# Theta from the attention output and a product of w_o and w_theta, with that output kept in DRAM

## The chip, the cores and the metric

The kernel runs on one core of a Trainium2 chip. The metric is the device time of one execution in microseconds; of several runs the median is given. Inputs and outputs lie in the core's DRAM; the host only lays arrays out.

## The reference

Three blocks follow each other, for four batches of 576 tokens and 512 channels. First, banded attention: eight heads of 64, each token looks at the 64 tokens up to itself. Second, four attention experts with causal masks over the result x, of which each token uses the two with the largest gate: `out = sum_e gate_e * (a_e @ v_e @ wo_e)`. Third, a mixing block over that output, called x again:

```
theta = x @ w_theta
zr, zi = x * cos(theta), x * sin(theta)
y = w_tok_r @ zr + w_tok_i @ zi        (over tokens)
u = x + y
out = u + max(u @ w_ch, 0)             (over channels)
```

The second block's output is linear in the gated attention outputs: with O of width 256 (four experts of 64) and w_o of 256 x 512, x = O w_o, and so theta = O (w_o w_theta). The first form contracts over 512, the second over 256.

## The kernel before

Everything is float32. A product is made from three matmuls (`mm3`, lines 92 to 95): each operand is split by `split` (lines 85 to 90) into a high part, rounded to the type fp32r, and the rest, and high x high, high x low and low x high are accumulated in one bank of PSUM. `split` uses two engines: ScalarE (ACT) casts the high part, and VectorE (DVE) or GpSimd (POOL) subtracts. TensorE writes to banks with the tags as, ta, g, bs and tb (one, one, two, two and two).

The program is written as generators that `merge` (line 45) interleaves by costs and totals (`KN`); the order of its text is the order of priority. A planner then sets the order of the instructions on every engine and queue with a simulated timeline (`schedule_with_timeline_sim`), so that work which is ready can go ahead of earlier text. Within an engine and within SP's queue of DMA issues the resulting order is fixed. Waits on the device follow from the tiles: a tile in a tag with one buffer can be written once all readers of the last tile of that tag are done.

The stages per batch b are: `phase_a(b)` is the banded attention, which loads q, k and v through SP (lines 231 to 248); `qk(b, ep)` and `vg_gates(b)` make the experts' q, k, v and gates; `attn(b, ep)` is the causal attention of a pair of experts, in five tiles t of tokens. Its result, already weighted by the gates and transposed (128 channels by 576 tokens), is split at line 487 into `oh` and `ol` (three buffers each). `wo(b)` multiplies with w_o and leaves the result in `x2T[b]`, 4 x 128 channels by 576 tokens. Attention of batch b is merged with phase_a of the next ones, wo of the one before and the conversion of the weights, which come as 64-bit floats and pass through ACT, DVE and POOL (`load64`).

The mixing block is in the last stages. `x_split(b)` (line 514) splits x2T[b] for tokens 0 to 511 into the eight tiles cx, casts on ACT, subtractions on POOL, and once per pair of batches gathers the last 64 tokens of both in `xt` and splits them. `theta(b, dh)` (line 527) goes over four token tiles of 128 (five where the pair's tail is due) for one half dh of the channels: per tile 12 matmuls of 256 columns against w_theta (`wth`, `wtl`), two transposes of x, then rounding on DVE, sine and cosine on ACT, and z with its split. `mix(b, dh)` sums over tokens in four banks, nine steps of 12 matmuls of 288 columns; four adds on DVE (line 599) empty the banks. `channel(b)` is the product with w_ch and the output's stores. `theta(b, 1)` is merged with `mix(b, 0)`, `theta(b+1, 0)` with `mix(b, 1)`; then comes `channel(b)`. `theta(0, 0)` is merged with `wo(3)`, the last part of the attention stages (line 712).

Of the kernel before, what the change touches and what calls it, by code (L numbers as in the profile page):

```python
# [11 lines left out]
F32 = mybir.dt.float32  # L12
# [45 lines left out]
def kernel(ctx, tc, qT, kT, vw, consts, w_in, w_o, w_th, w_tk, w_ch, outT):  # L58
# [10 lines left out]
    halfpi = cp.tile([P, 1], F32, name="halfpi")  # L69
    nc.gpsimd.memset(halfpi, math.pi / 2.0)  # L70

    wth = cp.tile([P, NC, DM], F32R, name="wth")
    wtl = cp.tile([P, NC, DM], F32R, name="wtl")
    x2T = {b: cp.tile([P, NC, S], F32, name=f"x2T{b}") for b in range(2)}

    BANKS = {"as": 1, "ta": 1, "g": 2, "bs": 2, "tb": 2}
# [330 lines left out]
    def attn(b, ep):  # L407
# [7 lines left out]
        for t in range(5):  # L415
# [69 lines left out]
                          pT[:, j, i, :m], start=(j == t - 1), stop=False)  # L485
            nc.tensor.matmul(o[:, :m], VD[ep][:, t].rearrange("p h d -> p (h d)"), pT[:, t, 0, :m], start=(t == 0), stop=True)
            split(oh[:, q0 : q0 + m], ol[:, q0 : q0 + m], o[:, :m], nc.scalar, nc.vector)
            yield 0.4 * (t + 1)

    def wo(b):  # L490
# [10 lines left out]

    HW = DM // 2
    NK0 = 5
    xtags = ["QS0", "QS1", "KA0", "KA1", "KL0", "oh", "ol", "KL1"]
    utags = ["QS2", "QS3", "KA2", "KA3", "oh", "ol", "oh", "ol"]
    XH, Z, UH, XT, W4 = {}, {}, {}, {}, 4 * P
    nz = [0]

    def hl_set(tags, name):
        t = [bp.tile([P, S], F32R, tag=tag, bufs=3 if tag in ("oh", "ol") else 1, name=f"{name}{i}")  # L510
             for i, tag in enumerate(tags)]
        return t[0::2], t[1::2]

    def x_split(b):
        XH[b] = hl_set(xtags, f"cx{b}")
        for c in range(NC):
            split(XH[b][0][c][:, :W4], XH[b][1][c][:, :W4], x2T[b][:, c, :W4], nc.scalar, nc.gpsimd)
        if b % 2 == 0:
            xt = kp.tile([P, NC, P], F32, tag="xt", name=f"xt{b}")
            for k in range(2):  # L520
                pool_mul(xt[:, :, 64 * k : 64 * k + 64], x2T[b + k][:, :, W4:], 1.0)
            xth = kp.tile([P, NC, P], F32R, tag="xth", name=f"xth{b}")
            xtl = kp.tile([P, NC, P], F32R, tag="xtl", name=f"xtl{b}")
            split(xth, xtl, xt, nc.scalar, nc.gpsimd)
            XT[0] = xt, xth, xtl

    def theta(b, dh):
        x2 = x2T[b]
        xh, xl = XH[b]
        dsl = slice(dh * HW, dh * HW + HW)  # L530
        for i in range(4 if b % 2 else 5):
            n = f"{b}{dh}{i}"
            if i < 4:
                tok = slice(i * P, i * P + P)
                x32, lh, ll = (lambda c: x2[:, c, tok]), (lambda c: xh[c][:, tok]), (lambda c: xl[c][:, tok])
            else:
                xt, xth, xtl = XT[0]
                x32, lh, ll = (lambda c: xt[:, c]), (lambda c: xth[:, c]), (lambda c: xtl[:, c])
            th = bank([P, HW], "bs", f"th{n}")
            for c in range(NC):  # L540
                mm3(th, lh(c), ll(c), wth[:, c, dsl], wtl[:, c, dsl], c == 0, c == NC - 1)
            xk = bank([P, HW], "tb", f"xk{n}")
            for c in range(2):
                nc.tensor.transpose(xk[:, c * P : (c + 1) * P], x32(2 * dh + c), ident)
            if i % 2 == 0:
                ang = bp.tile([P, 2, 2, HW], F32, tag="bms", bufs=2, name=f"ang{n}")
            rn, sn = ang[:, i % 2, 0], ang[:, i % 2, 1]
            nc.vector.tensor_scalar(out=rn, in0=th, scalar1=MAGIC, scalar2=-MAGIC,
                                    op0=ALU.add, op1=ALU.add)
            nc.vector.tensor_sub(out=rn, in0=th, in1=rn)  # L550
            nc.scalar.activation(out=sn, in_=rn, func=AF.Sin, scale=TWO_PI)  # L551
            nc.scalar.activation(out=rn, in_=rn, func=AF.Abs)
            nc.scalar.activation(out=rn, in_=rn, func=AF.Sin, bias=halfpi, scale=-TWO_PI)  # L553
            if i < 4:
                if b > 0 and nz[0] % NZ == 6:
                    zt = rp.tile([P, 2, 2, HW], F32R, tag="bmsx", name=f"z{n}")
                else:
                    pool, tag = ((cp, "zc"), (rp, "wtu"), (bp, "bpT"))[nz[0] % NZ % 6 // 2]
                    zt = pool.tile([P, 2, 2, HW], F32R, tag=tag, bufs=2, name=f"z{n}")
                nz[0] += 1  # L560
                if b > 0 and nz[0] < 14:
                    nz[0] = 14
                Z[b, dh, i] = zt
                for q, tr in enumerate((rn, sn)):
                    z = rp.tile([P, HW], F32, tag="z", bufs=2, name=f"zf{n}{q}")
                    nc.vector.tensor_mul(out=z, in0=xk, in1=tr)  # L566
                    split(zt[:, q, 0], zt[:, q, 1], z, nc.scalar, nc.gpsimd)
            else:
                for k in range(2):
                    zt = kp.tile([P, 1, 2, HW], F32R, tag=f"zt{k}{dh}", name=f"z{n}{k}")  # L570
                    Z[b + k, dh, i] = zt
                    z = rp.tile([P, HW], F32, tag="z", bufs=2, name=f"zf{n}{k}")
                    r = slice(64 * k, 64 * k + 64)
                    for q, tr in enumerate((rn, sn)):
                        nc.vector.tensor_mul(out=z[64 * q : 64 * q + 64], in0=xk[r], in1=tr[r])
                    split(zt[:, 0, 0], zt[:, 0, 1], z, nc.scalar, nc.gpsimd)
            yield 1.5
# [91 lines left out]
    for b in range(B):  # L669
        todo = [(KN["AT"][2 * b], attn(b, 0)), (KN["QK"][2 * b], qk(b, 1))]  # L670
        if KN["WOI"] == 2 * b:
            todo.append((KN["CW"][6], load_w(w_o, 2, lambda c: woh[c], lambda c: wol[c], "zc")))
        if b < B - 1:
            todo.append((KN["PA"][2 * b], phase_a(b + 1, range(KN["AS"][b + 1], 4))))
        if b > 0:
            todo.append((KN["WO"][b - 1], wo(b - 1)))
        if THS[2 * b]:
            todo.append((KN["TW"][0] * len(THS[2 * b]), load_theta(THS[2 * b])))
        if b == 3:
            todo.append((KN["TW"][2] * (NK0 - TK0), load_tok(range(TK0, NK0))))  # L680
        merge(*todo)
        if b == 2:
            ap.release()
            xp[0].release()
            rp = tc.alloc_tile_pool(name="rp", bufs=1, side="right", reuse_waits="tile")
            x2T[2] = rp.tile([P, NC, S], F32, name="x2T2")
            wkh = [rp.tile([P, S], F32R, name=f"wkh{c}") for c in range(NK0)]
            wkl = [rp.tile([P, S], F32R, name=f"wkl{c}") for c in range(NK0)]
        if b == 3:
            xp[1].release()  # L690
            wp.release()
            kp = tc.alloc_tile_pool(name="kp", bufs=1, side="left", reuse_waits="tile")
            x2T[3] = kp.tile([P, NC, S], F32, name="x2T3")
            wkh += [kp.tile([P, S], F32R, name=f"wkh{c}") for c in range(NK0, 9)]
            wkl += [kp.tile([P, S], F32R, name=f"wkl{c}") for c in range(NK0, 9)]
        todo = [(KN["AT"][2 * b + 1], attn(b, 1))]
        if b < B - 1:
            todo += [(KN["QK"][2 * b + 1], qk(b + 1, 0)), (KN["VG"][b + 1], vg_gates(b + 1))]
        if b < B - 2:
            todo.append((KN["PA"][2 * b + 1], phase_a(b + 2, range(KN["AS"][b + 2]))))  # L700
        if KN["WOI"] == 2 * b + 1:
            todo.append((KN["CW"][6], load_w(w_o, 2, lambda c: woh[c], lambda c: wol[c], "zc")))
        if THS[2 * b + 1]:
            todo.append((KN["TW"][1] * len(THS[2 * b + 1]), load_theta(THS[2 * b + 1])))
        if b == 2:
            todo.append((KN["TW"][3] * TK0, load_tok(range(TK0))))
        if b == 3:
            todo.append((KN["TW"][4] * (9 - NK0), load_tok(range(NK0, 5))))
        merge(*todo)
    merge((4, load_tok(range(5, 9))), (9, islice(wo(3), 0)))  # L710
    x_split(0)
    merge((KN["WO"][3], wo(3)), (KN["CW"][0], theta(0, 0)))
    wc = [bp.tile([P, DM], F32R, tag=f"wo{x}{c}", name=f"wc{x}{c}") for c in range(2) for x in "hl"]
    wd = [bp.tile([P, 2, DM], F32R, tag="vg", bufs=2, name=f"wd{c}") for c in range(2)]
# [3 lines left out]
    for b in range(B):  # L718
        todo = [(KN["TC"][4], mix(b, 0)), (KN["TC"][b % 2], theta(b, 1))]
        if b == 0:  # L720
            todo.append((KN["CW"][3], islice(ch, 3)))
        merge(*todo)
        if b < B - 1:
            x_split(b + 1)
            todo = [(KN["TC"][4], mix(b, 1)), (KN["TC"][2 + b % 2], theta(b + 1, 0))]
            if b == 0:
                todo.append((KN["CW"][3], ch))
            merge(*todo)
        else:
            merge((13, mix(b, 1)))  # L730
        merge((12, channel(b)))
# [55 lines left out]
```

## Time and profile before

| what | value |
|---|---|
| median of three runs | 526.95 us (525.98 to 527.31) |
| profiled execution: span, first to last instruction | 525.2 us |
| TensorE (PE) busy | 506.1 us, 96% of the span |
| weight loads of TensorE (PEld) | 476.3 us, 91% |
| VectorE (DVE), ScalarE (ACT), GpSimd (POOL) busy | 319.9, 329.8, 303.9 us |
| DMA | 36.80 MB |
| granted TensorE clock, mean | 0.997 of full speed |

The span lacks what lies around the first and last instruction, 1.75 us against the median. Weight loads run beside the matmuls. Ends of matmuls are modelled and overlap: a row's duration (0.28 us for 256 columns) is longer than the distance to the next matmul. Each stretch below is read by the starts.

### The profile page before, as it was taken

Reading aid. Unit: us, or ns where it says so; the run is one execution under the profiler, and the core shown is the slowest. Engines: PE = TensorE matmul, PEld = TensorE weight load, DVE = VectorE, ACT = ScalarE, POOL = GpSimd, SP = SyncE. Lnnn points to the kernel's source line nnn. Section 1 sums busy time; section 2 is a strip of 40 time slices with the busy share of each in tenths; the row PEclk is TensorE's granted clock in tenths of the full one; section 3 lists DMA queues with packets and bytes.
Section 4 is the critical chain, followed back from the end, with each engine's and each line's share of the span. In section 5 each row is a group of like instructions: output and inputs, shape, how many; then the busy total and the mean of one; then the engine's idle time right before and its main releaser. Section 6 shows DMA issues by size and latency. Waiting matters only on the chain.

```text
span 525.2 us, 12349 instructions
## 1 busy us (share of the span) xinstructions
PE 506.1 (96%) x4372; PEld 476.3 (91%) x4372; DVE 319.9 (61%) x1244; ACT 329.8 (63%) x1045; POOL 303.9 (58%) x464
## 2 busy tenths in 40 slices
PE   7799899999999999999888999999999999999997
PEld 5688888899998999989777999999999999999997
DVE  5756878757968778556988778453325324533312
ACT  7948778866978969677888977552437136523410
POOL 5667889754867833246885776951475227531420
PEclk9999999999999999999999999999999999999999
DMA  7573233322224331101304121002000200011002
GB/s 249 179 239 114 80 121 107 109 80 86 95 64 134 101 117 32 31 2 46 92 2 155 66 78 45 1 8 72 13 2 1 67 25 1 1 57 35 1 1 91
DMA packets 21086, 36.80 MB, mean 70 GB/s; under 512 B 2336, under 2 KB 13600, under 8 KB 21024
## 3 DMA queue, kind: packets, MB, share of 16 engines
q1 hardware_dynamic: 19008, 31.22, 18.4%
q10 hardware_dynamic: 2016, 4.79, 2.7%
q8 instruction: 35, 0.57, 0.5%
q14 instruction: 27, 0.22, 0.1%
HBM read 31.28 MB, written 4.72 MB: 69 GB/s over the span
## 4 chain that ended last, share of the span: by engine, by line
PE 79%; DVE 8%; ACT 7%; DMA 2%; issue 2%; POOL 1%; SPq 0%; ACTq 0%; POOLq 0%; DVEq 0%
PE y L93 7%; PE y L95 7%; PE y L94 7%; PE as L267 4%; PE c L95 3%; PE c L94 3%; PE c L93 3%; PE th L93 3%; PE th L94 3%; PE th L95 3%; PE bpt L468 3%; PE qk L93 3%; PE apt L292 2%; PE qk L94 2%; PE qk L95 2%; PE bs L436 2%
## 5 line engine op out<-in xcount | busy, mean ns | idle before, releaser
L90 POOL TENSOR_TENSOR z<-zf,z 128x256 fp32r<-128x256 f32 x72 | 53.1, 754 | 89.4 <-ACT z L87 89.3
L93 PE MATMUL y<-wkh,z 128*128 128x288 f32 x288 | 85.9, 300 | 0.3 <-ACT x2T L498 0.3
L94 PE MATMUL y<-wkl,z 128*128 128x288 f32 x288 | 84.9, 296 | 0.0
L95 PE MATMUL y<-wkh,z 128*128 128x288 f32 x288 | 83.6, 297 | 0.0
L280 ACT ACTIVATE ams<-ams,anm 128x128 f32<-128x128 f32 x144 | 56.6, 397 | 6.2 <-DVE anm L272 4.8
L93 PEld LDWEIGHTS y<-wkh,z 128*128 128x128 f32 x288 | 54.2, 188 | 0.6 <-ACT x2T L498 0.6
L287 POOL TENSOR_TENSOR ams<-ams,arc 128x384 f32<-128x384 f32 x48 | 40.1, 838 | 25.2 <-DVE arc L286 12.1
L94 PEld LDWEIGHTS y<-wkl,z 128*128 128x128 f32 x288 | 54.2, 188 | 0.0
L95 PEld LDWEIGHTS y<-wkh,z 128*128 128x128 f32 x288 | 53.5, 188 | 0.0
L82 POOL TENSOR_SCALAR QD<-qt 64x192 f32<-64x192 f32 x72 | 39.9, 555 | 19.5 <-PE as L267 13.1
L87 ACT CAST z<-zf 128x256 fp32r<-128x256 f32 x72 | 27.3, 403 | 36.7 <-DVE zf L566 15.3
L445 ACT ACTIVATE bms<-bms,bnm 64x64 f32<-64x64 f32 (+4 forms) x80 | 44.8, 562 | 7.3 <-DVE bnm L440 6.4
L267 PE MATMUL as<-kt,QD 128*128 128x128 f32 x288 | 42.6, 285 | 4.1 <-DVE anm L272 1.7
L551 ACT ACTIVATE ang<-ang 128x256 f32<-128x256 f32 x36 | 14.6, 415 | 50.8 <-DVE ang L550 50.7
L566 DVE TENSOR_TENSOR zf<-xk,ang 128x256 f32<-128x256 f32 x64 | 25.3, 419 | 34.1 <-ACT ang L553 19.4
L267 PEld LDWEIGHTS as<-kt,QD 128*128 128x128 f32 x288 | 37.3, 196 | 7.9 <-DVE anm L272 1.8
L272 DVE CUSTOM_DVE_ANT_0 ams<-as,cst 128x128 f32<-128x128 f32 x144 | 34.9, 283 | 11.5 <-PE apt L292 7.6
L440 DVE CUSTOM_DVE_ANT_0 bms<-bs,mb 64x64 f32<-64x64 f32 (+4 forms) x80 | 32.6, 422 | 7.4 <-PE bs L438 5.4
L93 PE MATMUL th<-wth,cx 128*128 128x256 f32 x128 | 36.2, 283 | 0.0
L94 PE MATMUL th<-wtl,cx 128*128 128x256 f32 x128 | 35.9, 281 | 0.0
L90 POOL TENSOR_TENSOR cu<-x2T,cu 128x288 fp32r<-128x288 f32 x32 | 25.5, 820 | 17.7 <-ACT cu L87 15.9
L95 PE MATMUL th<-wth,cx 128*128 128x256 f32 x128 | 35.6, 283 | 0.0
(198 smaller groups left out, 1735.1 us busy)
## 6 DMA issues: line engine op xcount, KB each, us to landing
vt<-in_dram SPq DMA_DIRECT2D x48, 192.0 KB, 3.2
kt<-in_dram SPq DMA_DIRECT2D x15, 320.0 KB, 2.9
qt<-in_dram SPq DMA_DIRECT2D x16, 288.0 KB, 3.3
out_dram<-x2T SPq DMA_DIRECT2D x32, 144.0 KB, 1.8
w64k<-in_dram SPq DMA_DIRECT2D x5, 576.0 KB, 3.7
w64k<-in_dram ACTq DMA_DIRECT2D x4, 576.0 KB, 3.6
w64t<-in_dram SPq DMA_DIRECT2D x4, 512.0 KB, 3.8
w64c<-in_dram ACTq DMA_DIRECT2D x8, 256.0 KB, 2.7
```

The costliest lines, as they stand in the source:

```text
L82: nc.gpsimd.tensor_scalar(out=out, in0=in_, scalar1=by, scalar2=1.0, op0=ALU.mult, op1=ALU.mult)
L87: nc.scalar.copy(out=dst_h, in_=src)
L90: eng_l.tensor_sub(out=dst_l, in0=src, in1=f32(dst_h))
L93: nc.tensor.matmul(out, wh, xh, start=first, stop=False)
L94: nc.tensor.matmul(out, wh, xl, start=False, stop=False)
L95: nc.tensor.matmul(out, wl, xh, start=False, stop=last)
L267: nc.tensor.matmul(s[:, i, :], QD[g][:, i], kt[:, 64 * blk : 64 * blk + 128], start=True, stop=True)
L272: nc.vector.tensor_tensor_reduce(out=ms[:, i, :], in0=s[:, i, :], in1=ma0 if (g == 0 and i == 0) else ma1, scale=-0.125, scalar=3.0e38, op ...
L280: nc.scalar.activation(out=ms[:, i, :], in_=ms[:, i, :], func=AF.Exp, bias=nm[:, i : i + 1], scale=-1.0, accum_out=sm[:, i, 0:1],)
L287: nc.gpsimd.tensor_mul(out=ms, in0=ms, in1=rc.unsqueeze(2).to_broadcast([P, 3, P]))
L440: nc.vector.tensor_tensor_reduce(out=ms[:m, a:z], in0=s[:m, : z - a], in1=mb[:m, mo + a : mo + z], scale=-0.125, scalar=nm[:m, 0:1] if ci ...
L445: ex = nc.scalar.activation(out=ms[:m, :w], in_=ms[:m, :w], func=AF.Exp, bias=nm[:m, ci : ci + 1], scale=-1.0, accum_out=ss[:m, i, 0:1])
```

## The change

Theta is no longer made from x2T. `attn` stores each oh and ol after its last tile to DRAM tiles `od[b]`, through SP. A new generator `fuse`, merged with the last `attn(3, 1)`, loads w_o in float32 into the tags KL0 and KL1, transposes it on TensorE (eight transposes of 128x128), splits it (ACT and DVE), multiplies it with wth and wtl (two banks of 512 columns, 12 matmuls each) and splits the result into tiles of the tags QS0, QS1, KA0 and KA1. `load_o(b)` takes the place of `x_split(b)`: for batches 0 to 2 it loads the four parts of O back, three into the space of wth or wtl and one into KL0 or KL1; batch 3's are still on the chip. The pair's tail is loaded from `od` into `xo`. `theta` has six matmuls per tile in place of 12. The tile `xt` and the transposes of x for z stay. u's tiles take KL2 and KL3 in place of one buffer each of oh and ol.

```diff
@@ tiles
+    dp = ctx.enter_context(tc.tile_pool(name="dp", bufs=1, space=bass.MemoryType.DRAM))
+    od = [dp.tile([P, 4, S], F32, name=f"od{b}") for b in range(B)]
+    wth = cp.tile([P, NC, DM], F32R, tag="wth", name="wth")
+    wtl = cp.tile([P, NC, DM], F32R, tag="wtl", name="wtl")
@@ attn
             split(oh[:, q0 : q0 + m], ol[:, q0 : q0 + m], o[:, :m], nc.scalar, nc.vector)
+            if t == 4:
+                for k, x in enumerate((oh, ol)):
+                    nc.sync.dma_start(od[b][:, 2 * ep + k], f32(x))
@@
-    xtags = ["QS0", "QS1", "KA0", "KA1", "KL0", "oh", "ol", "KL1"]
-    utags = ["QS2", "QS3", "KA2", "KA3", "oh", "ol", "oh", "ol"]
+    FUSE = 14.0
+    utags = ["QS2", "QS3", "KA2", "KA3", "KL2", "KL3", "oh", "ol"]
@@
-    def x_split(b):
-        XH[b] = hl_set(xtags, f"cx{b}")
-        for c in range(NC):
-            split(XH[b][0][c][:, :W4], XH[b][1][c][:, :W4], x2T[b][:, c, :W4], nc.scalar, nc.gpsimd)
+    def fuse():
+        woT = []
+        for e in range(2):
+            st = bp.tile([P, DM], F32, tag=f"KL{e}", name=f"wo32{e}")
+            with tc.issue_after(last_load[0].ins):
+                nc.sync.dma_start(st, w_o[e * P : (e + 1) * P])
+            pt = bank([P, NC, P], "g", f"woT{e}")
+            for j in range(NC):
+                nc.tensor.transpose(pt[:, j], st[:, j * P : (j + 1) * P], ident)
+            wt = [kp.tile([P, NC, P], F32R, tag=f"zt{e}{k}", name=f"woT{e}{k}") for k in range(2)]
+            split(*wt, pt, nc.scalar, nc.vector)
+            woT.append(wt)
+            yield 1.0
+        for e in range(2):
+            g = bank([P, DM], "g", f"wot{e}")
+            for c in range(NC):
+                mm3(g, woT[e][0][:, c], woT[e][1][:, c], wth[:, c], wtl[:, c], c == 0, c == NC - 1)
+                yield 0.7
+            gt = [bp.tile([P, DM], F32R, tag=f"{x}{e}", name=f"wot{x}{e}") for x in ("QS", "KA")]
+            split(*gt, g, nc.scalar, nc.vector)
+            GT[e] = gt
+
+    def load_o(b):
+        if b == B - 1:
+            O[b] = [O[b, c][k] for c in range(2) for k in range(2)]
+        else:
+            ow = cp.tile([P, 3, S], F32R, tag=("wth", "wtl")[b % 2], name=f"ow{b}")
+            ok = bp.tile([P, S], F32R, tag=f"KL{b % 2}", name=f"ok{b}")
+            nc.sync.dma_start(f32(ow), od[b][:, :3])
+            nc.sync.dma_start(f32(ok), od[b][:, 3])
+            O[b] = [ow[:, k] for k in range(3)] + [ok]
         if b % 2 == 0:
             xt = kp.tile([P, NC, P], F32, tag="xt", name=f"xt{b}")
+            xo = kp.tile([P, 4, P], F32R, tag="xo", name=f"xo{b}")
             for k in range(2):
                 pool_mul(xt[:, :, 64 * k : 64 * k + 64], x2T[b + k][:, :, W4:], 1.0)
-            xth = kp.tile([P, NC, P], F32R, tag="xth", name=f"xth{b}")
-            xtl = kp.tile([P, NC, P], F32R, tag="xtl", name=f"xtl{b}")
-            split(xth, xtl, xt, nc.scalar, nc.gpsimd)
+                nc.sync.dma_start(f32(xo[:, :, 64 * k : 64 * k + 64]), od[b + k][:, :, W4:])
@@ theta
-            for c in range(NC):
-                mm3(th, lh(c), ll(c), wth[:, c, dsl], wtl[:, c, dsl], c == 0, c == NC - 1)
+            for c in range(2):
+                mm3(th, ow[2 * c], ow[2 * c + 1], GT[c][0][:, dsl], GT[c][1][:, dsl], c == 0, c == 1)
@@ the main program, in the merge with attn(3, 1); load_o stands where x_split stood
+            todo.append((FUSE, fuse()))
...
-    x_split(0)
+    load_o(0)
```

## Rows read from the trace of the kernel before

**Rows 1.** Busy time by stretch: start:end, length, each engine (instructions), clock, DMA.
```profile
255.00:282.00 27.00, 24.68 (x189) 20.89 (x188) 23.29 (x79) 21.75 (x63) 22.01 (x27) 1.00 0.12 38
282.00:306.00 24.00, 21.95 (x191) 20.17 (x189) 19.59 (x46) 22.19 (x55) 15.46 (x13) 1.00 0.25 88
...
282.00:290.00 8.00, 6.34 (x56) 5.66 (x55) 7.55 (x22) 7.50 (x17) 5.30 (x5) 1.00 0.47 161
...
306.00:330.00 24.00, 24.00 (x187) 23.81 (x188) 19.33 (x50) 18.42 (x52) 17.33 (x24) 1.00 0.21 67
...
306.00:509.20 203.20, 203.20 (x1579) 202.89 (x1580) 87.33 (x216) 89.13 (x230) 96.35 (x123) 1.00 0.08 26
```

**Rows 2.** The page's chain of waits: shares of the span by engine.
```profile
PE 79%; DVE 8%; ACT 7%; DMA 2%; issue 2%; POOL 1%; SPq 0%; ACTq 0%; POOLq 0%; DVEq 0%
```

**Rows 3.** Busy time by stretch of the instructions on tile th: PE, PEld, DVE.
```profile
240.00:306.00 66.00, 10.28 (x72) 9.20 (x72) 3.13 (x8) 1.00 0.19 63
306.00:330.00 24.00, 6.84 (x50) 6.39 (x50) 4.62 (x12) 1.00 0.21 67
306.00:525.20 219.20, 49.72 (x360) 45.91 (x360) 26.55 (x64) 1.00 0.09 30
```

**Rows 4.** Timeline of PE: start, duration, instruction; matmuls of 320 and 256 columns.
```profile
300.35 0.31 PE L93 MATMUL x<-oh,woh 128*128 128x320 f32 x1
...
300.93 0.31 PE L94 MATMUL x<-ol,woh 128*128 128x320 f32 x1
...
324.31 0.28 PE L93 MATMUL th<-wth,cx 128*128 128x256 f32 x1
...
325.73 0.38 PE L544 MATMUL xk<-cst,x2T 128*128 128x128 f32 x2
...
326.06 0.28 PE L94 MATMUL th<-wtl,xth 128*128 128x256 f32 x1
```

**Rows 5.** Groups of instructions by shape: count, busy us, mean ns, idle before.
```profile
L90 POOL TENSOR_TENSOR cx<-x2T,cx 128x512 fp32r<-128x512 f32 x16 | 20.7, 1308 | 0.6 <-ACT cx L87 0.6
...
L87 ACT CAST cx<-x2T 128x512 fp32r<-128x512 f32 x16 | 9.5, 618 | 9.0 <-PE c L94 9.0
...
L470 DVE COPY bpT<-bpt 128x512 f32<-128x512 f32 x6 | 4.1, 686 | 0.4 <-PE bpt L468 0.4
```

**Rows 6.** Timelines of PE, POOL and DVE around the last attention.
```profile
265.89 0.29 PE L438 MATMUL bs<-KL,QS 128*128 128x288 f32 x1
...
270.41 1.41 POOL L133 TENSOR_TENSOR wkl<-wtuk,wkh 128x576 fp32r<-128x576 f32 x1
...
270.51 1.59 DVE L457 TENSOR_SCALAR bms<-bms,bsm,gw 128x512 f32<-128x512 f32 x1
...
272.32 0.69 DVE L457 TENSOR_SCALAR bms<-bms,bsm,gw 128x512 f32<-128x512 f32 x1
...
287.27 0.74 DVE L548 TENSOR_SCALAR ang<-th 128x256 f32<-128x256 f32 x2
...
303.76 0.28 DVE L90 TENSOR_TENSOR ol<-o,oh 128x128 fp32r<-128x128 f32 x1
```

**Rows 7.** DMA issues: count, KB each, median us from issue to landing.
```profile
w64k<-in_dram SPq DMA_DIRECT2D x5, 576.0 KB, 3.7
...
wst<-in_dram SPq DMA_DIRECT2D x2, 256.0 KB, 5.2
```

**Rows 8.** Timeline of DVE: the adds out of the banks, mix(0, 0).
```profile
325.07 1.17 DVE L599 TENSOR_TENSOR x2T<-y,x2T 128x288 f32<-128x288 f32 x3
327.04 0.45 DVE L599 TENSOR_TENSOR x2T<-y,x2T 128x288 f32<-128x288 f32 x1
```

**Rows 9.** Waits of SP's queue: us in total, times, longest.
```profile
SPq L248 <- PE ao L148: 95.1, 24, 12.4
```

**Rows 10.** Timeline of SP's queue: DMA issues.
```profile
70.40 0.33 SPq L234 DMA_DIRECT2D kt<-in_dram  x1
...
71.78 0.33 SPq L235 DMA_DIRECT2D qt<-in_dram  x1
```

More of the change, by code (lines that the diff above doesn't have):

```diff
@@ L70 @@
     nc.gpsimd.memset(halfpi, math.pi / 2.0)
-    wth = cp.tile([P, NC, DM], F32R, name="wth")
-    wtl = cp.tile([P, NC, DM], F32R, name="wtl")
+    dp = ctx.enter_context(tc.tile_pool(name="dp", bufs=1, space=bass.MemoryType.DRAM))
+    od = [dp.tile([P, 4, S], F32, name=f"od{b}") for b in range(B)]
+    wth = cp.tile([P, NC, DM], F32R, tag="wth", name="wth")
+    wtl = cp.tile([P, NC, DM], F32R, tag="wtl", name="wtl")
     x2T = {b: cp.tile([P, NC, S], F32, name=f"x2T{b}") for b in range(2)}
@@ L503 @@
     NK0 = 5
-    xtags = ["QS0", "QS1", "KA0", "KA1", "KL0", "oh", "ol", "KL1"]
-    utags = ["QS2", "QS3", "KA2", "KA3", "oh", "ol", "oh", "ol"]
-    XH, Z, UH, XT, W4 = {}, {}, {}, {}, 4 * P
+    FUSE = 14.0
+    utags = ["QS2", "QS3", "KA2", "KA3", "KL2", "KL3", "oh", "ol"]
+    Z, UH, XT, GT, W4 = {}, {}, {}, {}, 4 * P
     nz = [0]
@@ L520, in x_split @@
             for k in range(2):
                 pool_mul(xt[:, :, 64 * k : 64 * k + 64], x2T[b + k][:, :, W4:], 1.0)
-            xth = kp.tile([P, NC, P], F32R, tag="xth", name=f"xth{b}")
-            xtl = kp.tile([P, NC, P], F32R, tag="xtl", name=f"xtl{b}")
-            split(xth, xtl, xt, nc.scalar, nc.gpsimd)
-            XT[0] = xt, xth, xtl
+                nc.sync.dma_start(f32(xo[:, :, 64 * k : 64 * k + 64]), od[b + k][:, :, W4:])
+            XT[0] = xt, xo
     def theta(b, dh):
         x2 = x2T[b]
-        xh, xl = XH[b]
@@ L534, in theta @@
                 tok = slice(i * P, i * P + P)
-                x32, lh, ll = (lambda c: x2[:, c, tok]), (lambda c: xh[c][:, tok]), (lambda c: xl[c][:, tok])
+                x32, ow = (lambda c: x2[:, c, tok]), [o[:, tok] for o in O[b]]
             else:
-                xt, xth, xtl = XT[0]
-                x32, lh, ll = (lambda c: xt[:, c]), (lambda c: xth[:, c]), (lambda c: xtl[:, c])
+                xt, xo = XT[0]
+                x32, ow = (lambda c: xt[:, c]), [xo[:, k] for k in range(4)]
             th = bank([P, HW], "bs", f"th{n}")
-            for c in range(NC):
-                mm3(th, lh(c), ll(c), wth[:, c, dsl], wtl[:, c, dsl], c == 0, c == NC - 1)
+            for c in range(2):
+                mm3(th, ow[2 * c], ow[2 * c + 1], GT[c][0][:, dsl], GT[c][1][:, dsl], c == 0, c == 1)
             xk = bank([P, HW], "tb", f"xk{n}")
@@ L723 @@
         if b < B - 1:
-            x_split(b + 1)
+            load_o(b + 1)
             todo = [(KN["TC"][4], mix(b, 1)), (KN["TC"][2 + b % 2], theta(b + 1, 0))]
```

## The prediction, on record before the changed kernel ran

> **What bounds the kernel now.** I read the stretches by engine first. From 306 to 509.2 us, the part that makes theta, mixes tokens and mixes channels for the four batches, TensorE is busy in all of 203.2 us, while VectorE, ScalarE and GpSimd are busy for 87, 89 and 96 us, less than half [rows 1]. Then the chain of waits: 79% of it is TensorE [rows 2]. So there a matmul less is its time less, unless something else comes late. Ahead of it, from 255 to 306, the last attention, the conversion of the token weights and the first theta run together, and no engine is full: TensorE is idle for 2.3 and 2.05 us of the two stretches, but VectorE is busy for 7.55 of the 8 us from 282 to 290, where TensorE has 6.34 [rows 1]. The reader is to see two regimes: a long one bound by TensorE, and ahead of it 50 us of vector chains, in which work added to VectorE costs and work taken from TensorE need not pay.
>
> **The change, part by part.** Theta. It has 432 matmuls, 72 before 306 us and 360 after, 50 of these by 330 [rows 3]; the contraction halves, so 36 and 180 go. Twelve of them begin between 324.31 and 325.73 us, 1.42/12 = 0.118 us each [rows 4]. After 306: 180 x 0.118 = -21.3 us. Before: 36 x 0.118 = -4.3 us of TensorE time. The two transposes of a tile stay.
>
> The product (fuse) is new: 24 matmuls of 512 columns. No row has that width. Matmuls of 320 columns follow each other at (300.93 - 300.35)/4 = 0.145 us [rows 4], so a column costs (0.145 - 0.118)/64 = 0.00042 us and 512 columns 0.145 + 192 x 0.00042 = 0.225 us: an estimate, 24 x 0.225 = 5.4 us (lower bound 24 x 0.145 = 3.5). The eight transposes: from 325.73 to 326.06 stand a pair and one matmul, 0.33 - 0.12 = 0.21 a pair [rows 4], 0.85 us for four pairs. So +6.25 - 4.3 = +2.0 us of TensorE before 306, where 4.4 us are idle.
>
> The Trainium skill gives another price for the wide matmul ("TensorE: Matmul & The Clock Gate", section "Back-to-back issue gap"): about 131 ns sustained at 512 columns. By it the product would cost 3.1 us and the sum would be 2.3 us lower. The rows speak against it: 320 columns already take 145 ns [rows 4].
>
> Splits. The 16 ACT casts (0.62 us) and 16 POOL subtractions (1.31 us) of 128x512 into cx go [rows 5], and two of each of the same size for the tails. Those that theta of batch 0 needs, five and five, lie before 306: 3.1 us of ACT and 6.5 of POOL. In come four ACT casts of about the same size and four VectorE subtractions from a 512-wide bank; the copy of such a bank takes VectorE 0.69 us [rows 5], so 2.75 us. The rest of the splits lie after 306 beside a full TensorE: nothing gained.
>
> The start, up to 306 us. Its terms are TensorE +2.0, VectorE +2.75, ACT -0.7, POOL -6.5. The fuse can begin when attn(3, 0) has read KL0 and KL1 for the last time, about 266 us [rows 6]; a 256 KB load landed in 5.2 us [rows 7], so transposes about 271, splits 1.5 us, products mixed with attention until about 280, the second split 281. Only then is wth free for the load of ow0, 864 KB; 576 KB took 3.7 us [rows 7], so about 5.5: 286. VectorE takes the first theta tile at 287.27 us in the run before [rows 6]: the load is just in time, with about a microsecond to spare. I cost the start at +3 us, the VectorE work, because VectorE is the nearest to full there [rows 1]; the low end is -1 (POOL's and ACT's relief shortens the chains and the idle TensorE time hides the rest), the high end +10 (third case below).
>
> POOL's relief may be worth more than that. A VectorE scaling of 512 columns that began at 270.51, beside a POOL subtraction of 1.41 us, took 1.59 us; its like at 272.32 took 0.69 [rows 6]. That subtraction makes wkl and stays, but if each of the five removed ones held VectorE up by as much, the start would win 5 x 0.9 = 4.5 us. The Trainium skill ("SBUF — State Buffer", section "SBUF: two separate sides") says that the two engines lock a shared pair of ports and the loser waits out the whole instruction; the row agrees for one pair, and none shows it for the instructions that go.
>
> The first mix, 306 to 330. Here 25 matmuls go, 3.0 us of the 21.3. But VectorE is busy for 19.3 of the 24 us [rows 1]; squeezed to 21 us it would be 92% busy, as in 282 to 290, where TensorE had gaps. Between 0 and 3.0 of it is lost; I take 1.5, the middle.
>
> Boundaries. Between the last product of mix(b, 0) and the first of mix(b, 1) up to 24 theta matmuls cover VectorE's four adds out of the banks. For batch 0 the adds run from 325.07 to 327.49 [rows 8]; with 12 fewer matmuls the next mix could begin 1.4 us earlier and its fourth bank would be about 0.4 us late. The planner also fills with channel matmuls. 0 to 8 x 0.4 = 3.2; I take 0.5.
>
> Stores and loads. Eight pairs of stores stand in SP's queue, each waiting for the last split of an attn; behind them wait the loads of k, q and v for phase_a, and for these phase_a. SP already waits 95 us for v's buffers [rows 9], so its loads go out as buffers come free and a short wait ahead of them is hidden. The order of SP's queue isn't that of the program: the k load and the q load that the code issues back to back are issued at 70.40 and 71.78 us [rows 10], so the planner places what is ready, and a store should stand about where its data are. I take 0.5 us, between 0 and the fourth case. The loads of ow1 and ow2 have tens of microseconds and nothing waits.
>
> Sum: -21.3 + 3 + 1.5 + 0.5 + 0.5 = -15.8 us. The profiled span is 525.2 us, the median of the three runs 526.95, so 1.75 us lie around it: 525.2 - 15.8 + 1.75 = 511 us.
>
> **The rivals.** (1) The forecast: 507 to 515 us. Chance 0.55.
>
> (2) All that is added hides, and the start gets no longer: -21.3 with at most 1 to spare on either side, 504 to 507, or 502 where VectorE is also held up less by POOL, as above. For: 4.4 us of idle TensorE time [rows 1], and the 1.59 us in rows 6. Against: VectorE full from 282 to 290. Chance 0.21.
>
> (3) The first theta comes late, and the gap moves to the start: the load of ow0 stands in SP's queue behind the last store, whose data are split at 303.76 + 0.28 = 304 us [rows 6]. Then it lands at 309.5; the first z follows after six matmuls (0.7 us) and eight vector operations of 256 columns, taken at 0.5 us from the 512-column ones of rows 5, so the mix begins near 315 instead of 306: +9.5 in place of +3, 515 to 520; some microseconds of lateness in the w_o load, the bank g or the fuse end in between. For: the store comes ahead of the load in the program. Against: SP's order in rows 10. Chance 0.15.
>
> (4) Slower than before. A store pair waits at the head of SP's queue while loads for phase_a, whose buffers are free, wait behind it, and TensorE runs dry in the next phase_a. Six of the eight pairs (batches 0 to 2) have such loads behind them. At 5 us each, under half of the longest wait that SP has now (12.4 us) [rows 9], that is 30 us, less 15.8: 541 us. It decides from 15.8/6 = 2.6 us a pair. For: the 12.4 us waits show that SP does stand blocked. Against: they are waits for buffers, which no load could have used. Chance 0.05.
>
> (5) The change does not do what it says: vector chains pace the theta stages, TensorE only gets idle, and the time stays near 525 to 528. Against: under 50% load on the other three engines [rows 1]. Chance 0.04.
>
> **How the numbers follow.** The likeliest is (1), 511. From 503 to 519 lie all of (1), most of (2) and most of (3), about 0.83. A measurement of this kernel can tell about 0.3%, 1.6 us. Faster by more: (1), (2), (3), 0.91; within: (5), 0.04; slower: (4), 0.05.
>
> **What would show it.** In the profile after: 216 theta matmuls in place of 432 at 0.118 us, no cx and no GpSimd work for it; 24 fuse matmuls at 0.22 to 0.23 us between 270 and 282; the first y matmul at 308 to 310 (later than 315: case 3; 306 or before: case 2); from it to the end 22 us less than 219.2, less 1.5 to 3; TensorE without gaps from 330 on. k, q and v loads with waits on the od stores, or a first y matmul that has moved although the fuse came on time, would show (4). Wrong would be: TensorE idle after 330, or a saving there under 15 us.

## The result, and the profile after

The changed kernel takes 508.72 us (median, 508.37 to 509.75) against 526.77 us for the kernel before, run beside it: a ratio of 0.9663, 95% interval 0.9644 to 0.9682. The forecast was 511, its range 503 to 519. Its execution that was profiled has a span of 506.6 us, 18.6 us less than before.

The page of the changed kernel, busy time and then the chain of waits by engine [rows 2]:

```profile
PE 486.7 (96%) x4188; PEld 455.5 (90%) x4188; DVE 320.9 (63%) x1248; ACT 323.6 (64%) x1031; POOL 282.2 (56%) x446
...
PE 72%; ACT 8%; DVE 7%; DMA 6%; POOL 3%; issue 2%; SPq 0%; POOLq 0%; ACTq 0%; DVEq 0%
```

TensorE lost 19.4 of its 506.1 us and GpSimd 21.7 of 303.9; TensorE's share of the chain fell from 79 to 72%, and DMA rose from 2 to 6%. Where the time went is best seen by cutting both executions at the same events: the last matmul of the experts' q and k (tile qk), the first token-mixing matmul (y), the first channel matmul (c), the end. Busy time of the stretches between them (columns as in [rows 1]), kernel before:

```profile
268.40:305.90 37.50, 34.77 (x294) 31.01 (x292) 30.98 (x90) 31.50 (x86) 25.30 (x28) 1.00 0.24 78
305.90:348.70 42.80, 42.80 (x335) 42.48 (x335) 28.30 (x71) 29.29 (x81) 32.92 (x42) 1.00 0.12 38
348.70:525.20 176.50, 173.28 (x1343) 173.05 (x1340) 63.16 (x155) 60.97 (x152) 66.64 (x85) 1.00 0.08 28
```

and the changed kernel:

```profile
266.90:308.50 41.60, 38.55 (x291) 33.79 (x290) 31.80 (x94) 32.49 (x87) 20.77 (x23) 0.96 0.48 163
308.50:345.50 37.00, 37.00 (x289) 36.83 (x288) 29.36 (x72) 28.02 (x78) 27.59 (x38) 1.00 0.28 88
345.50:506.60 161.10, 157.79 (x1211) 157.55 (x1209) 63.21 (x154) 57.11 (x142) 55.90 (x76) 1.00 0.09 30
```

From the first c to the end 15.4 us are gone, and TensorE's busy time fell by the same (173.28 to 157.79): 22 theta tiles lie there, and 22 x 6 = 132 matmuls of 0.118 us are 15.6. From y to c, 5.8 us are gone, for eight tiles, 48 matmuls (5.7), and TensorE has no gap in either kernel. So from the first y on 21.2 us are saved: there every matmul left out paid its full price. Theta's own share (columns as in [rows 3]) is halved as it should be:

```profile
240.00:306.00 66.00, 5.54 (x36) 4.71 (x36) 3.28 (x8) 0.97 0.39 128
...
306.00:506.60 200.60, 27.58 (x180) 24.15 (x180) 26.38 (x64) 1.00 0.13 43
```

Ahead of the first y it is longer: 41.6 us in place of 37.5. Of these 4.1 us, 1.5 are not seen in the span: the kernel before was late by that much already (268.4 against 266.9). In this execution it ran 3.4 us near 66 us at half the clock, but that this is the whole reason is not shown. TensorE's columns split the 4.1: idle time grew by 0.3 (37.50 - 34.77 against 41.60 - 38.55). Busy time grew by 3.8, of which 1.7 is a lower clock (0.96 over 41.6 us) and 2.1 is left for work. This says what TensorE did in the stretch, not what set its length. What happened there, in windows of 1 us:

```profile
290.00:291.00 1.00, 0.37 (x2) 0.18 (x2) 1.00 (x1) 0.27 (x1) 1.00 (x2) 1.00 1.02 426
291.00:292.00 1.00, 0.82 (x3) 0.59 (x4) 0.76 (x4) 0.41 (x1) 1.00 (x2) 0.68 0.97 378
292.00:293.00 1.00, 1.00 (x5) 1.00 (x5) 0.36 (x3) 1.00 (x3) 0.03 (x1) 0.50 1.00 412
293.00:294.00 1.00, 1.00 (x6) 1.00 (x5) 1.00 (x2) 0.68 (x3) 0.90 (x1) 0.50 0.32 129
```

TensorE is busy in 0.37 of the microsecond from 290, and then its granted clock is 0.50 (1.2 of 2.4 GHz) until 294.7. The wait ahead of it is for VectorE, as the timelines of GpSimd, VectorE and TensorE show (a number in brackets is the idle time ahead of an instruction and its releaser):

```profile
289.51 1.40 POOL L129 TENSOR_TENSOR wtuk<-wtuk 128x576 int32<-128x576 int32 x1
289.53 1.60 DVE L459 TENSOR_SCALAR bms<-bms,bsm,gw 128x384 f32<-128x384 f32 x1
...
291.18 0.57 PE L470 MATMUL bpt<-cst,bms 128*128 128x128 f32 x2 [0.81 <-DVE bms L459]
```

A scaling of attention weights takes 1.60 us beside a GpSimd instruction of 1.40; a wider one, of 512 columns, took 0.54 at 294.99, when GpSimd was idle. It is the pair of which the prediction showed one case [rows 6]. No run tests whether the one instruction holds up the other. The DMA engines are full at the same time. The issues and ScalarE's timeline show what was late there:

```profile
284.08 0.80 SPq L547 DMA_DIRECT2D ow<-od  x2
...
293.34 0.74 ACT L119 ACTIVATE wtuk<-w64k 128x576 f32<-128x576 f32 x1 [0.32 <-DMA w64k<-in_dram]
```

The loads of ow0 and ow1 (864 KB each) go out together as soon as the product has read wth and wtl, up to half a microsecond ahead of a 576 KB piece of the token weights, which ScalarE's queue issues at 284.62. In the chain of waits that piece is the longest step of the start:

```profile
284.62 8.63 DMA w64k<-in_dram
```

It took 8.63 us, where such pieces took 3.7 before [rows 7] (3.6 on ScalarE's queue). ScalarE itself waited only 0.32 us for it, the number in brackets above. TensorE's timeline (start, duration) shows the product, the slow stretch and the first theta:

```profile
277.96 0.39 PE L95 MATMUL wot<-wth,woT 128*128 128x512 f32 x1
...
280.50 0.39 PE L97 MATMUL wot<-wth,woT 128*128 128x512 f32 x1
...
293.65 0.47 PE L97 MATMUL x<-oh,wol 128*128 128x320 f32 x1
293.91 0.47 PE L96 MATMUL x<-ol,woh 128*128 128x320 f32 x1
...
295.35 0.37 PE L95 MATMUL th<-wotQS,ow 128*128 128x256 f32 x1
```

Twelve product matmuls begin between 277.96 and 280.50: 2.54/11 = 0.231 us each. At half clock two matmuls of 320 columns begin 0.26 us apart, at full clock 0.145 [rows 4]. Theta begins at 295.4, where before it began at 282.0.

SP's queue, at last: the loads of ow (count, KB each, median us to landing), then its waits (total, times, longest):

```profile
ow<-od SPq DMA_DIRECT2D x3, 864.0 KB, 5.6
```
```profile
SPq L250 <- PE ao L150: 84.7, 26, 10.9
...
SPq L492 <- ACT wtuc L119: 22.0, 1, 22.0
...
SPq L492 <- ACT bpT L480: 17.1, 3, 12.9
```

The 5.6 us are the median; of the two loads issued together the later, ow0, for which theta's first weight load waits, took 8.6. The stores (line 492) do hold the queue: the wait of 22 us is for the last pair, issued at 306.61 and 307.09, behind which no load of phase_a stands; the longest wait ahead of an earlier store is 12.9 us. Phase_a's loads wait less than before (84.7 against 95.1 [rows 9]).

### The profile page after: what moved, and what is told of

Same layout as the page of the kernel before. It is cut to its first block, busy times and chain, and to the rows that moved or that the text cites. A ratio compares the mean times of both kernels' runs of the same rounds, so it can differ in the third digit from the quotient of the medians.

```text
span 506.6 us, 11999 instructions
## 1 busy us (share of the span) xinstructions
PE 486.7 (96%) x4188; PEld 455.5 (90%) x4188; DVE 320.9 (63%) x1248; ACT 323.6 (64%) x1031; POOL 282.2 (56%) x446
## 4 chain that ended last, share of the span: by engine, by line
PE 72%; ACT 8%; DVE 7%; DMA 6%; POOL 3%; issue 2%; SPq 0%; POOLq 0%; ACTq 0%; DVEq 0%
PE y L97 8%; PE y L95 8%; PE y L96 8%; PE c L96 3%; PE c L97 3%; PE c L95 3%; PE as L269 3%; DMA w64k<-in_dram 3%; ACT ams L282 3%; PE bpt L470 2%; PE qk L95 2%; PE apt L294 2%; PE qk L96 2%; PE qk L97 2%; DMA wst<-in_dram 2%
## 5 line engine op out<-in xcount | busy, mean ns | idle before, releaser
L269 PE MATMUL as<-kt,QD 128*128 128x128 f32 x288 | 41.5, 280 | 4.2 <-ACT x0h L89 1.3
L642 DVE SCALAR_TENSOR_TENSOR x2T<-c,x2T 128x288 f32<-128x288 f32 x32 | 14.4, 457 | 36.4 <-PE c L97 36.2
L459 POOL TENSOR_SCALAR bpd<-bms,bsm,gw 128x64 f32<-128x64 f32 (+1 forms) x47 | 21.6, 460 | 23.0 <-DVE bsm L452 10.5
L438 PE MATMUL bs<-KA,QS 128*128 128x288 f32 (+4 forms) x96 | 31.9, 341 | 0.8 <-DVE bnm L442 0.7
```

The costliest lines, as they stand in the source:

```text
L269: nc.tensor.matmul(s[:, i, :], QD[g][:, i], kt[:, 64 * blk : 64 * blk + 128], start=True, stop=True)
L438: nc.tensor.matmul(s[:m, : z - a], qs[:, q0 : q0 + m], ka[:, a:z], start=True, stop=False)
```

## The experiments

Ratios stand against the kernel before, run on the same chip; the changed kernel's is 0.9663 [0.9644, 0.9682]. Most fences below hold the line of the profiled execution from the last qk matmul to the first y: the second column is the length, the third TensorE's busy time, and the granted clock stands third from the end.

**VectorE's work doubled.** The prediction put the start's +3 us down to VectorE; so more of its work there should cost as much again.

```diff
             split(*wt, pt, nc.scalar, nc.vector)
+            nc.vector.tensor_sub(out=wt[1], in0=pt, in1=f32(wt[0]))
...
             split(*gt, g, nc.scalar, nc.vector)
+            nc.vector.tensor_sub(out=gt[1], in0=g, in1=f32(gt[0]))
```

> The changed kernel with the four VectorE subtractions of fuse (0.68 us each) made twice, +2.7 us of VectorE work before the first y. Theory V: VectorE sets the start, so 510.5 to 511.5 us against 508.7. Theory T: VectorE waits for data at that time anyway, 508.4 to 509.7.

```profile
266.90:307.50 40.60, 37.14 (x293) 32.25 (x292) 34.56 (x98) 31.21 (x83) 20.35 (x23) 1.00 0.52 176
```

507.61 us, 0.965 [0.9633, 0.9667]. VectorE works 2.8 us more in the stretch (34.56 against 31.80), and the time does not rise. The half clock near 291 us is missing in this execution; with 1.7 us for it the changed kernel's stretch would be 39.9 us, so the added work may cost up to an estimated 0.7 us, not 2.8. VectorE's added work is not what the start cost.

**The load of ow1 later.** The rival: ow0 and ow1 crowd out w64k. In the first kernel ow1 waits for the last store.

```diff
...
+            if b == 1:
+                with tc.issue_after(last_od[0].ins):
+                    nc.sync.dma_start(f32(ow), od[b][:, :3])
+                    nc.sync.dma_start(f32(ok), od[b][:, 3])
...
```

> The changed kernel with one edit: the load of ow1 and ok1 (batch 1) is issued on SP after the last store to od, at about 307 us, instead of beside ow0's at 284. Theory T (transfers: ow0, ow1 and the stores share the DMA engines with w64k, whose load took 8.6 us where ScalarE waited for it, and this sets the first y matmul): ow0 and w64k land 2 to 4 us earlier, the first y at 306 to 307.5 in place of 308.5, the time 506.5 to 507.5 us against 508.7. Theory V (VectorE: the four added subtractions, 2.75 us, set it): no change, 508.2 to 509.2.

510.74 us, 0.9719 [0.9703, 0.9735]: slower than the changed kernel, and outside both expectations. The load went out at 307.7 and met the channel weights. From ScalarE's timeline:

```profile
334.88 0.43 ACT L119 ACTIVATE w64c<-w64c 128x256 f32<-128x256 f32 x1 [3.60 <-DMA w64c<-in_dram]
```

ScalarE waited 3.6 us for a piece of them, and the first c came at 349.6 in place of 345.5. The first y came at 308.6, as in the changed kernel, but this is the slowest of the four executions (512.4 us), with 3.4 us at half the clock near 66 us. From y to c it needs 41.0 us in place of 37.0, with TensorE idle for 2.95: the collision had moved. In the second kernel ow1 waits for an exponential of the last attention's last tile, on ScalarE's queue.

```diff
...
+            if b == 1:
+                with tc.issue_after(last_exp[0].ins):
+                    nc.scalar.dma_start(f32(ow), od[b][:, :3])
+                    nc.scalar.dma_start(f32(ok), od[b][:, 3])
...
```

> The changed kernel, complete, with the load of ow1 and ok1 issued by ScalarE's queue after the last exponential of attention (about 292 us), between the loads of the token weights and those of the channel weights. Theory T (transfers side by side delay the conversion of the weights; ow1_late moved the collision to 308 us): no 8.6 us load of w64k, no wait of 3.6 us for w64c, the clock's fall at 291 us gone, 506 to 507.7 us against 508.7. Theory P (what differs between these kernels is the planner's order, not the transfers): 508 to 511 whatever the loads do.

```profile
266.80:308.00 41.20, 37.76 (x293) 32.51 (x291) 31.74 (x94) 32.47 (x87) 20.87 (x23) 1.00 0.50 166
```

507.55 us, 0.9659 [0.9637, 0.9681]. Most of theory T's signs came: the longest w64k load there is 6.2 us, ow0 lands in 5.5, theta begins at 290.0, and the clock does not fall in three of the four executions (507.34 to 507.67 us; the fourth, at a mean clock of 0.997, took 509.49). The time lies in T's range, but the interval overlaps the changed kernel's: no gain is shown.

**The DRAM path.** The stores alone, added to the kernel before:

```diff
...
+            if t == 4:
+                for k, x in enumerate((oh, ol)):
+                    nc.sync.dma_start(od[b][:, 2 * ep + k], f32(x))
```

> The kernel before with the 16 stores of oh and ol to DRAM added and read by nothing. The forecast cost them at 0.5 us: 526.5 to 527.5 against 526.8. If stores at the head of SP's queue held up the loads of phase_a (the prediction's fourth case): over 529. If the earlier start of the stretch before 250 us in the changed kernel (0.5 us) comes from a new plan alone: 526 to 526.5.

526.82 us, 1.0015 [1.0004, 1.0027]: 0.0015 x 526 = 0.8 us. That stores block phase_a's loads and cost 30 us falls.

The changed kernel without the loads back; in the second also without the stores:

```diff
...
-            O[b] = [ow[:, k] for k in range(3)] + [ok]
...
+        O[b] = [wkh[0], wkl[0], wkh[0], wkl[0]]
...
```

> The changed kernel with theta's left operand taken from a tile of the token weights on the chip, so that ow, ok and xo are not loaded back (theta is another product); the fuse, its splits and the stores to DRAM stay. The changed kernel gains 18.05 us, free_theta 21.4: 3.3 us to be found. Theory L (the loads back: late theta, transfers beside the weights' loads): 505.5 to 506.5 us against 526.6 before. Theory F (the fuse: its splits and its wait chain inside the last attention): 508 to 509.

> no_load_back without the 16 stores to DRAM as well; of the added work only the fuse is left. If the stores cost what they cost alone (0.8 to 1.0 us in stores_only): 0.5 to 1.2 us below no_load_back. Theory L: 504.8 to 505.8. Theory F: 507 to 508.5.

507.8 us, 0.9652 [0.9629, 0.9674], and 507.63 us, 0.9667 [0.9645, 0.9688]. The first:

```profile
267.00:307.40 40.40, 36.10 (x291) 32.26 (x290) 31.58 (x95) 32.28 (x87) 20.95 (x24) 1.00 0.31 102
```

Theta begins at 286.7 in place of 295.4 and the clock stays up, yet the first y comes only 1.1 us earlier, and TensorE is idle for 4.3 us in place of 3.05. Two of its four executions have a mean clock of 0.995 and 0.996 all the same, and take 508.65 and 508.3 us; the others take 507.3 and 506.2. The crowded loads are real (the longest w64k load here is 4.8 us), and what they cost is within the intervals.

**Theta halved, without the product.** The kernel before, all splits kept, with half of theta's sum:

```diff
-            for c in range(NC):
-                mm3(th, lh(c), ll(c), wth[:, c, dsl], wtl[:, c, dsl], c == 0, c == NC - 1)
+            for c in range(2):
+                mm3(th, lh(c), ll(c), wth[:, c, dsl], wtl[:, c, dsl], c == 0, c == 1)
```

> The kernel before with theta contracted over channels 0 to 255 only, which leaves half of theta's product out (216 matmuls less); no fuse, no stores, no loads back, all splits kept. Where the stretch before the first y is bound by other things than TensorE (theories T and V both): the 180 matmuls after it pay, 21.3 us, and the 36 before it nothing: 505 to 505.8 us against 526.8. If TensorE bound that stretch too: 25.6 us, 501.2. If the first mix or the boundaries gave part back, as the prediction had it (2 us): 507 to 507.5.

```profile
266.60:306.60 40.00, 34.35 (x258) 29.31 (x256) 31.54 (x89) 35.06 (x89) 26.11 (x29) 0.91 0.23 74
306.60:347.20 40.60, 38.02 (x286) 36.90 (x286) 30.60 (x74) 28.94 (x81) 32.95 (x43) 1.00 0.12 40
330.00:350.00 20.00, 18.89 (x146) 18.61 (x145) 11.77 (x29) 14.60 (x39) 18.47 (x24) 1.00 0.01 2
```

510.06 us, 0.9699 [0.9685, 0.9713]: slower than the changed kernel, though nothing was added. The second line, here and in the next two fences, is the stretch from y to c. In the third GpSimd is busy for 18.47 of 20 us and TensorE has gaps, which the changed kernel has not. Two kernels follow: the same with only the two groups split that are used, and one in which theta is another product of the same size, with no split, product, store or load.

```diff
-        for c in range(NC):
+        for c in range(2):
             split(XH[b][0][c][:, :W4], XH[b][1][c][:, :W4], x2T[b][:, c, :W4], nc.scalar, nc.gpsimd)
...
-            split(xth, xtl, xt, nc.scalar, nc.gpsimd)
+            split(xth[:, :2], xtl[:, :2], xt[:, :2], nc.scalar, nc.gpsimd)
...
```

> half_theta (510.06 us) with only the channels that its halved theta reads split: 8 of the 16 casts and subtractions into cx go, and half of the two tails. Theory S (the splits on GpSimd, busy 18.5 of 20 us from 330 to 350 in half_theta, hold up the first mix once theta is short; 2.6 us of idle TensorE time between first y and first channel matmul): 507 to 508.5. Theory P (half_theta lost its time to the order that the planner chose and to the half clock from 282 to 298): 509.5 to 511, or anything that its own idle time and clock explain.

```profile
268.30:305.00 36.70, 32.59 (x258) 28.00 (x257) 28.10 (x88) 29.13 (x80) 20.83 (x24) 0.95 0.24 80
305.00:343.20 38.20, 37.26 (x288) 36.80 (x286) 31.55 (x74) 29.21 (x82) 32.68 (x42) 1.00 0.13 42
```

```diff
-        XH[b] = hl_set(xtags, f"cx{b}")
-        for c in range(NC):
-            split(XH[b][0][c][:, :W4], XH[b][1][c][:, :W4], x2T[b][:, c, :W4], nc.scalar, nc.gpsimd)
+        XH[b] = [wkh[0], wkh[0]], [wkl[0], wkl[0]]
...
```

> The kernel before with theta's operands taken from a tile of the token weights that is on the chip early: contraction over 256, no split of x2T for theta, no fuse, no stores, no loads back (theta itself is replaced by another product). It prices what the changed kernel adds. Theory W (work: up to the first channel matmul TensorE's own work sets the time, with some 5 us of idle time that stays): 25.6 us less than before and no product to pay, 6 to 8 us under the changed kernel's 508.7, so 500.5 to 502.5. Theory C (chains of the last attention set the first y matmul, TensorE's work there is free): first y at 305 to 306, the time 504.5 to 505.5.

```profile
268.30:304.50 36.20, 31.52 (x261) 26.95 (x259) 30.57 (x89) 29.86 (x82) 18.07 (x21) 1.00 0.25 81
304.50:344.50 40.00, 37.70 (x288) 36.80 (x287) 31.05 (x74) 28.19 (x78) 29.62 (x40) 1.00 0.12 40
```

505.52 us, 0.96 [0.9577, 0.9623], and 505.18 us, 0.9598 [0.958, 0.9616]. So product, stores and loads together cost 508.72 - 505.18 = 3.5 us; by the intervals of the two ratios it is 3.4, give or take 1.4. The lines show that this is a difference of two larger numbers: without them the start is 5.4 us shorter (36.2 against 41.6), but the first mix 3.0 us longer (40.0 against 37.0). There TensorE waits 0.9 us for the last copy of x (ScalarE), 0.9 for z (GpSimd) and 0.4 for zf (VectorE). (This execution is the slowest of its five, 507.19 us; its clock falls near 65 us, ahead of both stretches.) So an earlier first y is not worth its full length.

The 4.5 us between the two halved kernels look like the price of the splits, but ScalarE's timeline of the first (510.06 us) has something else in it:

```profile
286.11 1.28 ACT L551 ACT_TABLE_LOAD   x1
...
288.83 1.28 ACT L445 ACT_TABLE_LOAD   x1
...
291.01 1.28 ACT L551 ACT_TABLE_LOAD   x1
```

Line 551 is theta's sine, line 445 attention's exponential. The first sine stands ahead of the last exponential, so the function table is loaded three times, 1.28 us each; the kernel with half the splits has one load in that stretch, as have the kernel before and the changed one. Two more are 2.6 us of ScalarE, and TensorE lost clock besides (0.91 against 0.95). The start of the two differs by 3.3 us, so these can hold all of it; the stretch from y to c differs by 2.4 (40.6 against 38.2). One of TensorE's waits there, 1.11 us, is ended by GpSimd, as the splits would have it; but the kernel that splits nothing of x2T needs 40.0 us for the same stretch. That the splits are the cause is not shown.

**The product's matmuls.** 18 of the 24 left out:

```diff
-                mm3(g, woT[e][0][:, c], woT[e][1][:, c], wth[:, c], wtl[:, c], c == 0, c == NC - 1)
+                if c == 0:
+                    mm3(g, woT[e][0][:, c], woT[e][1][:, c], wth[:, c], wtl[:, c], True, True)
```

> The changed kernel with 18 of the 24 matmuls of the product left out (three of the four chunks of channels), 18 x 0.231 = 4.2 us of TensorE work less before the first y; splits, stores and loads stay. Theory W: 504 to 505.5 us against 508.7. Theory C: no gain, 508 to 509.5.

```profile
267.60:308.30 40.70, 34.90 (x275) 30.53 (x274) 34.44 (x94) 31.76 (x88) 19.80 (x23) 0.96 0.50 173
```

508.53 us, 0.9656 [0.9637, 0.9676]. In the stretch TensorE is busy for 3.65 us less and idle for 2.75 more, and the time is the same. The clock blurs this: three of the four executions have a mean clock of 0.992 or 0.993, where the changed kernel has 0.996 or 0.997; the one at 0.997 took 507.53 us. So a microsecond may have been won, not 4.2.

The same 24 placed otherwise in the merge:

```diff
-    FUSE = 14.0
+    FUSE = 20.0
```

> The changed kernel with the product placed later among the last attention's instructions (FUSE 20 in place of 14), the same work. All theories: the same sum. If the clock's fall from 291 to 295 us comes from TensorE's gaps ahead of it, another order can miss it: 507 to 507.5 without the fall, 508.4 to 509 with it.

508.68 us, 0.9667 [0.9648, 0.9687]: the same. Last, the short product and no loads back together, since each alone might leave the other as the limit:

```diff
...
-            O[b] = [ow[:, k] for k in range(3)] + [ok]
...
+        O[b] = [wkh[0], wkl[0], wkh[0], wkl[0]]
...
-                mm3(g, woT[e][0][:, c], woT[e][1][:, c], wth[:, c], wtl[:, c], c == 0, c == NC - 1)
+                if c == 0:
+                    mm3(g, woT[e][0][:, c], woT[e][1][:, c], wth[:, c], wtl[:, c], True, True)
```

> 18 of the 24 product matmuls are left out, and neither ow0, ow1 nor the blocks for the class token are loaded back (theta reads other data in their place); the stores stay. Theory J, two chains side by side: the product's two bursts hold the last attention (its last hi part at 306.3 us in the changed kernel, 302.3 without the bursts), and the loads beside w64k hold the first theta (295.4, and 286.7 without them). The first y needs both, so each edit alone moved it by about a microsecond or less. With both gone it starts at 304.5 to 305.5, and the time is 504.8 to 505.8, as where theta was another product (505.2). Rival O, the order in which the planner puts the work, or something else that every variant with the product shares: the first y stays at 307 to 308.5, and the time is 507 to 508.5.

```profile
267.10:309.50 42.40, 36.20 (x274) 31.52 (x272) 29.34 (x92) 34.19 (x88) 17.69 (x21) 0.92 0.30 98
```

509.48 us, 0.9679 [0.965, 0.9707]: the gain did not come, and the first y is later than ever. Theta begins at 282.2, early enough to get ahead of the last exponential again. ScalarE's timeline, then TensorE's:

```profile
289.01 1.28 ACT L573 ACT_TABLE_LOAD   x1
...
292.30 1.28 ACT L447 ACT_TABLE_LOAD   x1
...
294.37 0.56 ACT L474 COPY bpT<-bpt 128x512 f32<-128x512 f32 x1
294.95 1.28 ACT L573 ACT_TABLE_LOAD   x1
```
```profile
294.98 0.81 PE L150 MATMUL o<-bpT,vg 128*64 128x128 f32 x8 [2.04 <-ACT bpT L474]
```

TensorE waits 2.04 us for a copy that ScalarE makes behind the reloaded exponential, and right after that its clock falls. So this run says that an early theta is no gain by itself, but not whether the two chains do hold each other: the order on ScalarE changed along with them. Its six executions fall apart by the mean clock: 507.53 to 508.60 us at 0.999 to 1.000, 510.36 to 511.68 at 0.990 to 0.993. The three at the higher clock are 1.7 us and more over theory J's range too.

## Why the prediction was right

**Theta, -21.3 us after the first y.** Right in mechanism and size: 21.2. In that stretch TensorE was full before, and stayed full, but for some 3 us near the end in both kernels.

**First mix +1.5, boundaries +0.5.** Neither came: from y to c TensorE is busy for 37.00 of 37.00 us, with VectorE at 29.36 of them. These 2 us are most of the 2.3 by which 511 was too high. The fear was not empty: in the three kernels in which theta is halved and the first y comes earlier, TensorE is idle there for 0.9, 2.3 and 2.6 us. What spared the changed kernel is not shown. The relief of GpSimd (27.59 against 32.92) came in the same stretch, and the prediction had given it no value there; but the kernel without any of these splits has the gaps too.

**The start, +3.** The size was right and the reason wrong, so its agreement is luck. Measured +4.1 from the last qk matmul, +2.6 in the span's time. The step that failed is "I cost the start at +3 us, the VectorE work": the doubled subtractions, 2.8 us more of it, cost an estimated 0.7 us at the most. By TensorE's columns the 4.1 are the work that the prediction had worked out (+2.0, 2.1 by the profile) and set against 4.4 us of idle time, 1.7 us from a stretch at half clock, and 0.3 of idle time. The idle time did not shrink (2.7 before, 3.05 after): it is made of waits for attention's chains, and the work did not fill them. But that TensorE's work sets the length is not shown either: with 3.65 us of it taken out, idle time grew by 2.75.

**Theta "just in time" at 287.** Wrong: 295.4. The product ended at 284.1, not 280, and the split of its result at 287.6; then ow0 had to share the DMA engines with ow1 and w64k, which the prediction priced as if alone. It took 8.6 us; with ow1 issued later it took 5.5, the predicted figure. It cost little, because theta was not the last thing that the first y waited for: the last of wo(3) was, whose last matmul begins 0.3 us (changed kernel) and 0.8 us (before) ahead of the first y. So case (3), a late theta, did not become +9.5.

**Stores and loads, +0.5.** Right: 0.8 us for the stores alone, and without stores and loads a difference that the intervals don't show. Case (4) is refuted.

**The product.** 0.231 us a matmul against 0.225 estimated from two rows. The Trainium skill's 131 ns at 512 columns ("TensorE: Matmul & The Clock Gate", section "Back-to-back issue gap") does not hold for these matmuls.

**Left open.** Which part of product, stores and loads makes the 3.5 us over the kernel without any of them. Each part taken away alone moved the time by under 1.2 us, and the pair was spoilt by the table loads. The clock has a share: all four executions of the changed kernel have a mean clock of 0.996 or 0.997. In each of the six kernels that keep the whole product and have executions on both sides, those at 0.999 or more are in the mean 0.5 to 2.0 us faster than those at 0.995 to 0.997. So an estimated half to two of the 3.5 us may go with the clock. How far GpSimd's instructions slow VectorE's in attention's chains was not tested. A kernel that keeps the first sine behind the last exponential by its dependences was not tried. None of the complete versions (ow1 later, another place in the merge) is shown to beat the changed kernel.

## What to carry to other kernels

Where one engine is full and stays full, count the instructions that go and multiply by their distance in the trace: that term was exact to 0.1 us. Where no engine is full, idle time is no reserve: here TensorE's idle time stayed when work was added to it, work removed from it turned mostly into waiting, added VectorE work hardly showed, and each edit also moved the order in which the planner interleaves two chains. An earlier start can also come back as gaps in the stage behind it. Before calling a part dear because its removal gained time, compare what else changed places: table loads and granted clock first.

## What the runs showed of the hardware

A ScalarE table load takes 1.28 us, and the number of them went with the order of work: one between 262 us and the first mix in all other kernels here, three in two of them (510.06 and 509.48 us), in which a sine stands ahead of the last exponential. The Trainium skill ("ScalarE: Activation LUTs", section "Table sets: the hidden batching unit") says to batch activations by table set; the traces agree, with 2.6 us of ScalarE for one exponential that came late. That this makes the whole difference in time is read from the traces and was not isolated by a run.

A 576 KB load took 8.63 us, against 3.7, when two loads of 864 KB had been issued up to half a microsecond ahead of it on another queue; the longest such load was 6.2 us with one of the two and 4.8 with neither. So separate queues did not separate the transfers. The loads of ow are not the only cause: in the kernel with the short product and no loads back one took 6.9.

A VectorE scaling of 384 columns took 1.60 us beside a GpSimd instruction of 1.40 that had begun 0.02 us ahead of it, and TensorE waited 0.81 us for it. The kernel with FUSE 20 shows the same pair, 1.60 beside 1.40, and a wait of 1.34. The traces show the pairs; no run isolates them.

TensorE's granted clock fell to 0.50 after gaps in the start, in some kernels and some executions; 3.4 us at that level cost an estimated 1.7 us (half of the stretch), more than most of the edits tried here moved the time.
